# Two-step attention and a routed expert layer on one core: squared lengths off TensorE, PSUM banks given out singly, 1 MB stores and another order

## The chip, the core and the metric

The kernel runs on one core of a Trainium2 chip. The core has five engines that run side by side and each take their instructions in order: TensorE (PE; its weight loads are listed as PEld), VectorE (DVE), ScalarE (ACT), GpSimd (POOL) and SyncE (SP), which here only issues DMA transfers. ScalarE issues DMAs too. The working memory SBUF has 128 partitions; matmuls write to PSUM, eight banks of 512 float32 for each partition. The metric is the device time of one execution in microseconds (us).

## What is computed

```
h   = softmax(scale * I  @ x^T) @ x          # per batch b: 32 inducing rows over 11456 tokens
out = softmax(scale * x  @ h^T) @ h          # per token: over the 32 rows of h
xn  = out / (|out| + 1e-6);  en = emb / (|emb| + 1e-6)
logits = xn @ en^T / tau;    e = argmax(logits)      # 8 experts
gate   = softmax(logits)[e]
result = gate * (relu(out @ w1[e]) @ w2[e])
```

There are 4 batches of 11456 tokens with 128 channels, and 8 experts with a hidden width of 1024. Everything is float32.

## The kernel before

**What it works on.** A batch is cut into six pieces k of 2048 tokens (the last one of 1280). `xT` holds a piece with the channels on the partitions (1 MB), `x` holds it with the tokens on the partitions (two halves of 512 KB). For three pieces of batch 0 (`OWN`, `own`, line 345) x is not loaded but made on the chip from xT by transposes.

**Stage 1** (`stage1`, line 365) is the first softmax. For one or two pieces: scores by TensorE (`scores1`), a running maximum on VectorE (`mk`, `nb`), exponentials on ScalarE, transposes on TensorE, a copy on ScalarE, and the matmuls with x (line 448), added up in `hj`. `finish` (line 463) combines the four row groups into h transposed (`hT`, lines 514 to 520), finds the likeliest expert from the sum of the rows of h, has its weights w1 and w2 loaded by SyncE (`load`, line 543), and calls `tables`, which makes `HB` (the products of the rows of h with each other) and `gbd` (the products of the rows of h with the normalised expert vectors, in columns of a weight matrix, beside a column of ones).

**Stage 2** (`stage2`, line 587) is done for each piece k, 16 tiles of 128 tokens: scores (line 604), the maximum over 32 rows and its spreading by two transposing instructions (`mx`, `mxb`, lines 611 and 614), the difference (line 619), the exponential e (line 622). The length of an output token needs the sum over rows of e times (HB e). So TensorE computes HB e (line 623), VectorE multiplies it with e into `q` (line 625), and TensorE adds q up with the weights `nnb` into the same bank in which it adds e up with the weights `gbd` (function `half`, lines 630 and 631; two matmuls each). One transposing copy `gat` (line 643) brings the sums back with the tokens on the partitions, in `gts`.

**The gate** (`gate`, line 648) follows after three, two or one pieces (`GATES`): inverse square root by logarithm and exponential with one Newton step on GpSimd, logits, softmax, argmax. It is a chain of some fifteen small operations that goes to and fro between VectorE, ScalarE and GpSimd, and it ends in `f`, the factor of each token. If every hidden unit keeps its sign over all tokens, w1 and w2 fold into one matrix `L` for each batch (`fold`, line 748); `check` (line 815) tests whether that holds, and collects what has to be done again.

**Stage 3** (`stage3`, line 890): f is spread (line 873, VectorE), multiplied with e (line 875, GpSimd: `pf`), multiplied with L (line 901, TensorE, four matmuls into two PSUM tiles `pc` of two banks), copied out in halves (line 914, ScalarE) and stored in halves of 512 KB (`put`, line 884, issued by ScalarE).

**Order.** The whole program is a straight list of instructions whose order a planner sets while the program is built (`Plan`, line 77). Every step is added with an engine, an assumed duration, its dependences, the buffers it takes and frees, and a priority: the slot's time plus a constant of the stage (`PA`, `PT`, `PX`, `PC`, `PF`, `PD`). `run` picks, again and again, the step that can begin first; on one engine those that can begin within 0.2 us of each other go by priority. Buffers are rings (`BUFS`): the next user of a ring gets the oldest buffer. PSUM is two such rings, `pb` (four single banks) and `pc` (two pairs). Where TensorE would wait over 0.6 us for work that has a buffer already, matmuls on zeros are put in (`fill`, line 977).

**Behind the plan**, `worklist` (line 938) makes the list of what has to be done again, its count is read into registers on every engine (line 1055), and a loop over the list follows (line 1059). For the inputs here the list is empty, and the loop's body isn't run.

## Time and profile before

| | |
|---|---|
| median of three runs | 270.82 us (269.31 to 272.33) |
| the profiled execution | 271.37 us, of which its span 269.7 us |
| TensorE in the chain that ended last | 45% of the span |
| transfers in that chain | 22% |
| VectorE in that chain | 20% |
| moved by DMA | 72.29 MB, 268 GB/s on average |
| read from HBM, written | 48.13 MB, 23.72 MB |

The profile's first part gives each engine's busy time, share and number of instructions. The slices divide the span into 40 equal parts; a digit is tenths, and PEclk is the clock granted to TensorE. A row of stretches gives, for each piece of time, its length, the busy time of each engine with the number of instructions, the granted clock (1.00 is full speed), the share of the DMA engines and the GB/s that they moved. A row of instruction groups reads: line, engine, operation, what is written from what with its shape, the count, then busy us and mean ns, then the engine's idle time before these instructions and what ended it. A timeline row gives start, length, engine, line, and in brackets the idle time before it. A float32 matmul leaves two records, so "x8" stands for four matmuls.

### The profile page before, as it was taken

What the parts mean: (1) busy time and instruction counts of PE and PEld (TensorE: products, weight loads), DVE (VectorE), ACT (ScalarE), POOL (GpSimd) and SP (SyncE); (2) the same over time, 40 slices, a digit from 0 to 9 for tenths busy, and PEclk for the clock granted to TensorE, in tenths of its full rate; (3) what the DMA queues carried; (4) which work ended last, traced back from release to release, by engine and by line L of the source; (5) the groups of instructions that cost most, each with busy time, mean ns of one, the idle gap of its engine ahead of it and who ended that gap; (6) DMA issues with size and microseconds to landing.
All of it is one profiled execution on the core that took longest, in us unless ns stands there. A gap on an engine that the chain in (4) does not pass through costs nothing.

```text
span 269.7 us, 5435 instructions
## 1 busy us (share of the span) xinstructions
PE 225.8 (84%) x1993; PEld 122.0 (45%) x1993; DVE 179.1 (66%) x524; ACT 105.5 (39%) x227; POOL 68.9 (26%) x128
## 2 busy tenths in 40 slices
PE   8989899589968999999499998977996899786540
PEld 2557454246535256654273645633631564342220
DVE  5545247943897667979369869589589637958520
ACT  2355330131411472263016542666465720155430
POOL 2000000000440114641001353623257204263700
PEclk9999999979996699999959999999999799999755
DMA  6999998994781999859919998274579640037460
GB/s 187 397 419 384 399 377 317 402 395 159 260 304 36 314 382 418 364 203 368 419 53 277 385 417 359 85 293 172 214 231 417 255 173 0 0 156 289 173 252 17
DMA packets 18690, 72.29 MB, mean 268 GB/s; under 512 B 2456, under 2 KB 2976, under 8 KB 16224
## 3 DMA queue, kind: packets, MB, share of 16 engines
q1 hardware_dynamic: 11392, 48.37, 48.1%
q10 hardware_dynamic: 7264, 23.49, 21.8%
q8 instruction: 18, 0.29, 0.4%
q14 instruction: 16, 0.13, 0.2%
HBM read 48.13 MB, written 23.72 MB: 266 GB/s over the span
## 4 chain that ended last, share of the span: by engine, by line
PE 45%; DMA 22%; DVE 20%; ACT 4%; issue 3%; POOL 2%; ACTq 1%; DVEq 0%; POOLq 0%
DMA xT<-in_xT 18%; PE pc L901 9%; PE pb L630 6%; PE pb L631 5%; PE pb L604 5%; PE pb L623 5%; PE pb L448 4%; PE pc L331 3%; ACT o L914 3%; DMA out<-o 3%; PE pc L426 2%; DVE fb L873 2%; DMA itau<-in_tau 2%; DVE mk L388 2%; DVE gm L479 1%
## 5 line engine op out<-in xcount | busy, mean ns | idle before, releaser
L914 ACT COPY o<-pc 128x512 f32<-128x512 f32 (+1 forms) x94 | 48.3, 564 | 37.5 <-PE pc L901 26.8
L875 POOL TENSOR_TENSOR pf<-e,fb 128x512 f32<-128x512 f32 (+1 forms) x24 | 29.0, 1214 | 36.6 <-PE pc L901 14.8
L901 PE MATMUL pc<-pf,L 32*128 32x512 f32 (+1 forms) x192 | 32.7, 669 | 6.7 <-ACT o L914 3.9
L623 PE MATMUL pb<-e,HB 128*128 128x512 f32 (+1 forms) x48 | 25.0, 603 | 3.7 <-ACT o L914 2.2
L622 ACT ACTIVATE e<-d 128x512 f32<-128x512 f32 (+1 forms) x24 | 14.5, 603 | 23.1 <-DVE R L619 16.6
L331 PE MATMUL pc<-xT,indT_sb 128*32 128x512 f32 x120 | 16.6, 639 | 8.0 <-DMA xT<-in_xT 7.9
L604 PE MATMUL pb<-xT,hT 128*32 128x512 f32 x160 | 21.6, 640 | 0.0
L403 ACT ACTIVATE s<-pc,nb 128x1024 f32<-128x1024 f32 (+1 forms) x9 | 9.5, 1058 | 29.2 <-DVE nb L395 19.2
L643 DVE STREAM_TRANSPOSE gts<-pb 128x256 f32<-128x256 f32 (+1 forms) x24 | 10.3, 428 | 15.1 <-PE pb L631 14.9
L611 DVE TRANSPOSE_TENSOR_REDUCE mx<-pb 128x16 f32<-128x512 f32 (+1 forms) x24 | 16.1, 671 | 5.7 <-PE pb L604 5.7
L448 PE MATMUL pb<-x,pt 128*32 128x128 f32 x608 | 19.6, 274 | 0.1
L448 PEld LDWEIGHTS pb<-x,pt 128*32 128x32 f32 x608 | 16.0, 110 | 7.9 <-issue 3.2
L901 PEld LDWEIGHTS pc<-pf,L 32*128 32x128 f32 x192 | 10.7, 198 | 18.8 <-issue 10.2
L625 DVE TENSOR_TENSOR q<-pb,e 128x512 f32<-128x512 f32 (+1 forms) x24 | 15.4, 644 | 4.5 <-PE pb L623 4.3
L630 PE MATMUL pb<-q,nnb 128*128 128x256 f32 (+1 forms) x48 | 15.7, 410 | 1.8 <-DVE q L625 1.4
L614 DVE STREAM_TRANSPOSE mxb<-mx 128x512 f32<-128x512 f32 (+1 forms) x24 | 16.1, 670 | 0.4
L619 DVE CUSTOM_DVE_ANT_0 d<-mxb,pb 128x512 f32<-128x512 f32 (+1 forms) x24 | 15.5, 646 | 1.2
L388 DVE TENSOR_REDUCE mk<-pc 128x1 f32<-128x1024 f32 (+1 forms) x9 | 10.2, 1139 | 8.9 <-PE pc L331 8.0
L630 PE MATMUL pb<-e,gbd 128*128 128x256 f32 (+1 forms) x48 | 15.5, 407 | 0.4 <-DVE R L619 0.4
L873 DVE STREAM_TRANSPOSE fb<-f 128x512 f32<-128x512 f32 (+1 forms) x24 | 15.4, 658 | 0.3
L631 PE MATMUL pb<-e,gbd 128*128 128x256 f32 (+1 forms) x48 | 14.6, 387 | 0.0
L631 PE MATMUL pb<-q,nnb 128*128 128x256 f32 (+1 forms) x48 | 14.4, 384 | 0.0
(202 smaller groups left out, 359.7 us busy)
## 6 DMA issues: line engine op xcount, KB each, us to landing
out<-o ACTq DMA_DIRECT2D x40, 512.0 KB, 3.0
xT<-in_xT SPq DMA_DIRECT2D x19, 1024.0 KB, 12.4
x<-in_xP SPq DMA_DIRECT2D x38, 512.0 KB, 10.4
xL<-in_xT SPq DMA_DIRECT2D x4, 640.0 KB, 12.9
w1t<-in_w SPq DMA_DIRECT2D x4, 512.0 KB, 4.6
w2t<-in_w SPq DMA_DIRECT2D x4, 512.0 KB, 5.8
out<-o ACTq DMA_DIRECT2D x4, 320.0 KB, 2.5
out<-o ACTq DMA_DIRECT2D x4, 288.0 KB, 2.5
```

Source lines behind the costliest of these rows:

```text
L331: nc.tensor.matmul(ps[32 * j:32 * j + 32, :].rearrange("p (g i) -> p g i", i=128), lhsT=indT_sb, rhs=v[:, j], start=True, stop=True)
L448: nc.tensor.matmul(ph.t[32 * j:32 * j + 32, 0:C], lhsT=pt.t[:tw, tat[k] + g, 32 * j:32 * j + 32], rhs=x, start=k == ks[0] and g == 0, stop ...
L604: nc.tensor.matmul(ps[32 * j:32 * j + 32, :W].rearrange("p (t i) -> p t i", i=32), lhsT=st.hT[:, 0:M], rhs=v[:, j], start=True, stop=True)
L611: nc.vector.tensor_reduce(t["mx"][:, :T], b1.t[:, :W].rearrange("p (t i) -> p t i", i=32), AX.X, ALU.max, apply_transpose=True)
L614: c(DVE, t_dve(W), lambda: nc.vector.transpose(new(mxb)[:, :W], t["mx"][:, :T].unsqueeze(2).broadcast_to([P, T, 32])), take=[mxb])
L623: o = c(PE, t_pe(W), lambda: nc.tensor.matmul(new(b2)[:, :W], lhsT=st.HB, rhs=e.t[:, :W], start=True, stop=True), take=[b2], deps=[st.do.g ...
L630: nc.tensor.matmul(b3.t[:, :H], lhsT=w[:, 16:], rhs=src.t[:, :H], start=kw["start"], stop=False)
L631: nc.tensor.matmul(b3.t[:, :H], lhsT=w[:, :P], rhs=src.t[:, H:W], start=False, stop=kw["stop"])
L873: c(DVE, t_dve(W), lambda: nc.vector.transpose(new(fb)[:, :W], st.f[k].unsqueeze(3).broadcast_to([P, 2, T // 2, 32])), take=[fb], deps=[st ...
L875: c(POOL, t_pool(W), lambda: nc.gpsimd.tensor_tensor(new(pf)[:, :W], st.e[k].t[:, :W], fb.t[:, :W], ALU.mult), take=[pf], free=[fb, st.e[k]])
L901: nc.tensor.matmul(pcs[j // 2].t[:, 512 * (j % 2):512 * (j % 2) + W], lhsT=st.L[32 * j:32 * j + 32, :], rhs=pf.t[32 * j:32 * j + 32, :W], ...
L914: (nc.vector.tensor_copy if dve else nc.scalar.copy)(v[:, 2 * i:2 * i + 2], src)
```

## The change

1. **Squared lengths.** q and its two matmuls with `nnb` are gone. ScalarE copies HB e from PSUM to SBUF (`keep_hq`), GpSimd multiplies it with e (`times`), and VectorE adds it up over 32 rows with a transposing sum (`squared`) straight into a buffer `nn`. The sums with `gbd` and `gat` stay, and no longer wait for q.
2. **The gate.** Its steps get their own dependences instead of one chain, and each waits in the plan for the same step of the gate before. nn's lower bound goes from VectorE to ScalarE (a Relu and a bias `tiny`), the sum `se` goes from one VectorE reduction to three additions on GpSimd (but for the last gate).
3. **The fold.** `Gm` is made on GpSimd (`chosen`), the sides' small sums `pa`, `na` on VectorE; they were the other way round.
4. **PSUM.** One tile of eight banks; the planner gives out single banks, or two neighbouring ones, to each user (`banks_for`). Stage 3 takes four single banks, and each copy frees one.
5. **Stores** of a whole piece (1 MB, 24 in all) from two buffers of 1 MB. The store of hT goes from SyncE's queue to ScalarE's.
6. **Order.** Every step has a name; its priority is the slot's time plus a number for that name from a table (`FIRST`), and from the last batch on a second one (`LATE`). The 0.2 us of choice becomes a number for each engine (`NEAR`). Steps of batch 0's first stage and its finish get priorities far below all others. Assumed durations are changed slightly. Waits for buffers that the plan hadn't known are added as dependences: `get_w` waits for the fold before, `seen` for the last check, `fix` for hj three steps before.
7. **The end.** The work list becomes steps of the plan. The loop stands in the else branch of a test for an empty list, with a branch hint.

The diff's core:

```diff
-BUFS = dict(xT=7, xL=2, x=6, xR=1, s1=2, pt=1, mxb=2, d=2, e=7, q=2, gts=2, lg=2, ex=1, fb=2, pf=2, o=4, pb=4, pc=2)
+BUFS = dict(xT=7, xL=2, x=6, xR=1, s1=2, pt=1, mxb=2, d=2, e=7, hq=2, gts=2, lg=2, ex=1, fb=2, pf=2, o=2, mx=2, nn=2, f=3)
+BANKS = 8
...
+NEAR = dict(PE=0.1, Activation=0.5, DVE=0.1, SP=1.5, Pool=0.7)
...
+        o.prio = when + FIRST.get(o.name, 0.0) + (LATE.get(o.name, 0.0) if when >= T0 + (NB - 1) * NSB * SLOT else 0.0)
...
+    def banks_for(self, o, t):
+        free = {i: at for i in range(BANKS) for at in [self.bank_at(i)] if at is not None}
+        out = []
+        for b in o.take:
...
+            for i in range(BANKS - b.n + 1):
+                if not all(i + j in free for j in range(b.n)):
+                    continue
+                at = max(free[i + j] for j in range(b.n))
+                near = sum(1 for j in (i - 1, i + b.n) if j in free and free[j] <= max(t, at))
+                key = (max(t, at), near, -at, i)
+                if best is None or key < best[0]:
+                    best = (key, i, at)
...
-        c(DVE, t_dve(W), lambda: nc.vector.tensor_tensor(new(q)[:, :W], b2.t[:, :W], e.t[:, :W], ALU.mult), take=[q], free=[b2])
...
-        c(PE, t_pe(W) + 0.1, lambda: half(nnb, q, start=False, stop=True), deps=[o], free=[q])
...
+        def keep_hq():
+            nc.scalar.copy(paired(new(hq)[:, :W]), halved(b2.t[:, :W]))
+        c(ACT, t_act(W), keep_hq, take=[hq], free=[b2])
+        def times():
+            nc.gpsimd.tensor_tensor(paired(hq.t[:, :W]), paired(hq.t[:, :W]), halved(e.t[:, :W]), ALU.mult)
+        c(POOL, t_pool(W), times)
+        def squared():
+            nc.vector.tensor_reduce(new(nn)[:, t0:t0 + T], hq.t[:, :W].rearrange("p (t i) -> p t i", i=32), AX.X, ALU.add,
+                                    apply_transpose=True)
+        o_nn = c(DVE, t_dve(W), squared, take=[nn] if t0 == 0 else [], free=[hq])
...
-            nc.vector.tensor_scalar(t["nn"], col(NC, 1)[:, :, 0], 1e-30, None, ALU.max)
...
+            nc.scalar.activation(t["nn"], nn.t[:, :T], AF.Relu)
+            nc.scalar.activation(t["r"], t["nn"], AF.Ln, bias=tiny)
...
-            nc.vector.tensor_reduce(se, t["ex"], AX.X, ALU.add)
...
+            nc.gpsimd.tensor_tensor(x[:, :, 0:4], x[:, :, 0:4], x[:, :, 4:8], ALU.add)
+            nc.gpsimd.tensor_tensor(x[:, :, 0:2], x[:, :, 0:2], x[:, :, 2:4], ALU.add)
+            nc.gpsimd.tensor_tensor(t["se"], x[:, :, 0], x[:, :, 1], ALU.add)
...
-            nc.vector.tensor_tensor(st.Gm, st.G, pos.unsqueeze(2).broadcast_to([P, NCH, M]), ALU.mult)
...
-            nc.gpsimd.tensor_tensor(pa, sa, ss, ALU.add)
-            nc.gpsimd.tensor_tensor(na, sa, ss, ALU.subtract)
...
+            nc.gpsimd.tensor_tensor(st.Gm, st.G, t["pos"].unsqueeze(2).broadcast_to([P, NCH, M]), ALU.mult)
...
+            nc.vector.tensor_tensor(pa, sa, t["ss"], ALU.add)
+            nc.vector.tensor_tensor(na, sa, t["ss"], ALU.subtract)
...
-        pcs = [plan.buf("pc") for _ in range(2)]
+        pcs = [plan.buf("ps") for _ in range(4)]
...
+        o = plan.buf("o")
+        for j in range(4):
+            def evict(j=j, dve=split and j % 2 == 1):
+                v = new(o)[:, :P * T].rearrange("c (t j i) -> c j t i", j=4, i=32)
+                (nc.vector.tensor_copy if dve else nc.scalar.copy)(v[:, j], pcs[j].t[:, :W].rearrange("c (t i) -> c t i", i=32))
...
+        st.do["out", k] = plan.add(ACT, 0.34, put_o, deps=ops, free=[o], when=when, size=P * P * T * 4)
...
-    ni = worklist()
-    n_items = nc.values_load(ni, min_val=0, max_val=NB * E)
+    n_items = nc.values_load(left["ni"], min_val=0, max_val=NB * E)
...
-    with tc.For_i(0, n_items, 1) as i:
+    tc.mark_branch_hint_location("none", "LikelyTaken", engines=ENGINES)
+    with tc.If(n_items == 0, preferred_fallthrough_block=False, label="none") as none:
+        pass
+    with none.Else():
+        with tc.For_i(0, n_items, 1) as i:
```

More of the change, by code (lines that the diff above doesn't have):

```diff
@@ L114, in ready_at @@
                 return None
-            t = max(t, d.end + (0.0 if d.eng == o.eng and not d.size else self.HOP))
+            t = max(t, d.end + (0.0 if d.eng == o.eng and not d.size else self.HOP + d.lag))
+        o.room = 0.0
         want = {}
-        o.room = 0.0
         for b in o.take:
+            if b.ring == "ps":
+                continue
             live = self.rings.setdefault(b.ring, [])
@@ L152, in run @@
             for b in o.take:
-                self.rings[b.ring].append(b)
+                if b.ring != "ps":
+                    self.rings[b.ring].append(b)
+            for b, i, _ in o.got if o.take and o.take[0].ring == "ps" else ():
+                b.at = i
+                for j in range(b.n):
+                    self.banks[i + j] = b
             for b in o.free:
@@ L498, in finish, with fin @@
         c(DVE, 0.2, zf)
[L499 removed]
+        def fin():
+            nc.tensor.matmul(new(b3)[:, 0:1], lhsT=flat(sel4), rhs=t["z"], start=True, stop=True)
+        c(PE, 0.3, fin, take=[b3])
         def selr():
@@ new lines, in expB, with hb @@
+        def expB():
+            nc.scalar.activation(new(e)[:, :W], d.t[:, :W], AF.Exp, scale=-SCALE)
+        o_e = c(ACT, t_act(W), expB, take=[e], free=[d])
+        def hb():
+            nc.tensor.matmul(new(b2)[:, :W], lhsT=st.HB, rhs=e.t[:, :W], start=True, stop=True)
+        c(PE, t_pe(W), hb, take=[b2], deps=[st.do.get("tab")])
+        halved = lambda v: v.rearrange("p (u t i) -> p t u i", u=2, i=32)
+        paired = lambda v: v.rearrange("p (t u i) -> p t u i", u=2, i=32)
+        def keep_hq():
+            nc.scalar.copy(paired(new(hq)[:, :W]), halved(b2.t[:, :W]))
@@ L640, in gat @@
+            nc.tensor.matmul(b3.t[:, :H], lhsT=st.gbd[:, :P], rhs=e.t[:, H:W], start=False, stop=True)
+        o = plan.add(PE, t_pe(W), sums, deps=[o_e, st.do.get("tab")], take=[b3], when=when)
         def gat():
@@ L690, in newton @@
                 nc.gpsimd.tensor_tensor(t["n"], t["n"], t["p"], ALU.mult)
-        c(*((DVE, 3 * dv()) if last else (POOL, 4 * po)), newton)
+        o_n = add(*((DVE, 3 * dv()) if last else (POOL, 4 * po)), newton, deps=[o_r])
         def den():
@@ L697, in den @@
             nc.vector.reciprocal(t["den"], t["den"])
-        c(DVE, dv() + 0.43, den)
+        o_d = add(DVE, dv() + 0.5, den, deps=[o_z, o_n])
         def lg():
@@ L702, in lg @@
             nc.gpsimd.tensor_tensor(t["lg"], col(0, E), b8(t["den"]), ALU.mult)
-        c(POOL, t_pool(E * T), lg, take=[lgb], free=[gts])
+        o_l = add(POOL, 0.12 + 0.00172 * E * T, lg, deps=[o_d], take=[lgb], free=[gts])
         def lm():
@@ L825, in check, with chk @@
         c(DVE, 0.2, rm, deps=[st.do["R", k] for k in range(NSB)])
-        c(PE, 0.3, lambda: nc.tensor.transpose(new(b1)[0:1, 0:P], t["rm"], ident), take=[b1])
+        def chk():
+            nc.tensor.transpose(new(b1)[0:1, 0:P], t["rm"], ident)
+        c(PE, 0.2, chk, take=[b1])
         def r1():
@@ L872, in weighted @@
         fb, pf = plan.buf("fb"), plan.buf("pf")
-        c(DVE, t_dve(W), lambda: nc.vector.transpose(new(fb)[:, :W], st.f[k].unsqueeze(3).broadcast_to([P, 2, T // 2, 32])), take=[fb],
-          deps=[st.do.get(("f", k))])
-        c(POOL, t_pool(W), lambda: nc.gpsimd.tensor_tensor(new(pf)[:, :W], st.e[k].t[:, :W], fb.t[:, :W], ALU.mult), take=[pf],
-          free=[fb, st.e[k]])
-        return pf
-    def halves(k):
-        h = n_tiles(k) // 2
-        return [(0, h), (h, h)]
-    def put(st, k, o, a, h):
-        lap = LAP if k == NSB - 1 and a == 0 else 0
-        t0 = FULL * k if k < NSB - 1 else NTOK - LAST
-        st.put(t0 + P * a + lap, P * h - lap, o[:, lap:P * h])
@@ L890, in stage3, with spread_f, weigh, put @@
-    def stage3(plan, st, k, prio, split=False):
+        def spread_f():
+            nc.vector.transpose(new(fb)[:, :W], st.f[k].unsqueeze(3).broadcast_to([P, 2, T // 2, 32]))
+        c(DVE, t_dve(W), spread_f, take=[fb], free=[st.fv[k]], deps=[st.do.get(("f", k))])
+        def weigh():
+            nc.gpsimd.tensor_tensor(new(pf)[:, :W], st.e[k].t[:, :W], fb.t[:, :W], ALU.mult)
+        c(POOL, t_pool(W), weigh, take=[pf], free=[fb, st.e[k]])
+        return pf
+    def put(plan, st, k, o):
+        lap = LAP if k == NSB - 1 else 0
+        t0, n = (FULL * k, FULL) if k < NSB - 1 else (NTOK - LAST, LAST)
+        st.put(t0 + lap, n - lap, o[:, lap:n])
@@ L903, in stage3 @@
[L903 to L918 removed]
+                nc.tensor.matmul(new(pcs[j])[:, :W], lhsT=st.L[32 * j:32 * j + 32, :], rhs=pf.t[32 * j:32 * j + 32, :W], start=True, stop=True)
```

658 lines of the change are left out of this document (369 added, 289 removed).

## The prediction

> **What bounds the kernel now.** I read the page's busy times and slices first, then the busy times of five stretches that I cut by what the work is, then the waits and the timeline where a stretch shows a hole.
>
> ```profile
> span 269.7 us, 5435 instructions
> ...
> PE 225.8 (84%) x1993; PEld 122.0 (45%) x1993; DVE 179.1 (66%) x524; ACT 105.5 (39%) x227; POOL 68.9 (26%) x128
> ...
> PEclk9999999979996699999959999999999799999755
> ```
>
> TensorE is busy for 84% of the span. The share alone doesn't say where it is the limit, because part of it is filler (line 977: matmuls on zeros that keep the clock up). The stretches do:
>
> ```profile
> core 0: us, PE busy (x) PEld busy (x) DVE busy (x) ACT busy (x) POOL busy (x), PEclk, DMA share, GB/s
> ...
> 39.80:84.50 44.70, 37.68 (x388) 21.25 (x388) 32.28 (x79) 9.88 (x21) 6.78 (x12) 0.94 0.75 280
> 84.50:195.00 110.50, 101.27 (x945) 55.95 (x949) 83.23 (x226) 49.55 (x106) 33.51 (x57) 0.93 0.76 289
> 195.00:226.00 31.00, 26.61 (x160) 13.50 (x163) 20.80 (x55) 16.21 (x36) 11.53 (x22) 0.94 0.63 237
> 226.00:262.40 36.40, 24.22 (x129) 11.35 (x121) 24.44 (x80) 14.33 (x32) 15.15 (x25) 0.87 0.39 155
> 262.40:269.70 7.30, 0.00 (x0) 0.00 (x0) 0.00 (x0) 0.00 (x0) 0.00 (x0) 0.50 0.16 47
> ```
>
> Up to 39.8 us batch 0 is loaded and its first attention step ends. From 39.8 to 226 ("the middle", 186.2 us) stage 2 and 3 of one batch run beside stage 1 of the next. There TensorE is busy for 165.6 us. Only 0.8 us of it is filler:
>
> ```profile
> 84.50:195.00 110.50, 0.81 (x3) 0.29 (x3) 0.93 0.76 289
> ```
>
> So real TensorE work fills 164.8 / 186.2 = 88.5% of the middle. VectorE follows with 136.3 us (73%), then the transfers: shares 0.75, 0.76 and 0.63 make 137 us (74%). From 226 us on no engine is full, and the gate's steps and the last outputs wait for each other. The last 7.3 us hold no compute instruction at all. The executed run took 271.4 us, 1.7 around its span; the median of the runs, 270.8, is 0.2% less, so I sum against 271.4.
>
> **The change part by part.**
>
> *The squared lengths leave TensorE.* The two matmul pairs on q with the weights nnb (lines 630 and 631) go. In the middle they hold, by stretch:
>
> ```profile
> 39.80:84.50 44.70, 5.55 (x20) 3.56 (x20) 0.00 (x0) 0.00 (x0) 0.94 0.75 280
> 84.50:195.00 110.50, 13.98 (x52) 9.41 (x52) 0.00 (x0) 0.00 (x0) 0.93 0.76 289
> 195.00:226.00 31.00, 4.63 (x16) 3.28 (x16) 0.00 (x0) 0.00 (x0) 0.94 0.63 237
> ```
>
> That is 24.2 us, and leaves TensorE 140.6 us of work in the middle. If TensorE stayed the limit at 88.5%, the middle would take 158.9 us: 27.3 us less. That is the far end of the gain, because other engines get the work:
>
> ```profile
> L914 ACT COPY o<-pc 128x512 f32<-128x512 f32 (+1 forms) x94 | 48.3, 564 | 37.5 <-PE pc L901 26.8 <-ACT o L914 7.8 <-DMA out<-o 2.8
> ...
> L875 POOL TENSOR_TENSOR pf<-e,fb 128x512 f32<-128x512 f32 (+1 forms) x24 | 29.0, 1214 | 36.6 <-PE pc L901 14.8 <-DVE q L625 7.6 <-PE pb L554 5.8
> ...
> L611 DVE TRANSPOSE_TENSOR_REDUCE mx<-pb 128x16 f32<-128x512 f32 (+1 forms) x24 | 16.1, 671 | 5.7 <-PE pb L604 5.7
> ...
> L625 DVE TENSOR_TENSOR q<-pb,e 128x512 f32<-128x512 f32 (+1 forms) x24 | 15.4, 644 | 4.5 <-PE pb L623 4.3
> ...
> L864 POOL TENSOR_TENSOR seen<-seen 128x192 f32<-128x192 f32 (+3 forms) x16 | 6.2, 387 | 1.3
> ...
> L735 DVE TENSOR_REDUCE se<-ex 128x48 f32<-128x384 f32 (+3 forms) x9 | 4.3, 476 | 0.0
> ...
> L665 DVE TENSOR_SCALAR nn<-gts 128x48 f32<-128x48 f32 (+3 forms) x9 | 2.0, 221 | 0.3
> ...
> L779 DVE TENSOR_TENSOR Gm<-G,pos 128x256 f32<-128x256 f32 x4 | 1.8, 454 | 0.1
> ```
>
> ScalarE copies the product out of PSUM 24 times; by the eviction's 564 ns that is 13.5 us. GpSimd multiplies it with e 24 times, by the 1214 ns of its other multiplication of that size 29.1 us. VectorE drops q (644 ns) and takes the transposed sum "squared" (by mx, 671 ns): 24 x 27 ns = +0.6. It also drops nn (2.0) and the sum se, except the last one (about 4.1); six of nine gates lie in the middle, so 6/9 x 6.1 = -4.1. Gm goes to GpSimd: -1.8. The sums of se become three GpSimd additions, by line 864's mean 3 x 0.39 = 1.2 us for each of eight gates. pa and na come from GpSimd to VectorE, eight small operations of about 0.16 (the row of line 858 below): +1.3. GpSimd ends near 69 + 29 + 9 = 107 us and ScalarE near 119: half of a shorter span, so neither is the limit by its sum.
>
> *GpSimd's operations hold up VectorE's.* This is in the trace already:
>
> ```profile
> 77.79 1.27 POOL L875 TENSOR_TENSOR pf<-e,fb 128x512 f32<-128x512 f32 x1 [2.48 <-DVE fb L873]
> ...
> 77.90 1.24 DVE L479 COPY gm<-gm 1x128 f32<-1x128 f32 x1
> ...
> 118.48 0.88 POOL L875 TENSOR_TENSOR pf<-e,fb 128x320 f32<-128x320 f32 x1
> ...
> 118.58 0.84 DVE L696 SCALAR_TENSOR_TENSOR den<-zz,n 128x48 f32<-128x48 f32 x1
> ```
>
> A copy of one row takes 1.24 us and ends with the multiplication on GpSimd beside it; so does the short den. Two such pairs cost VectorE about 1.6 us over what an instruction this small needs (the 0.16 of line 858). With 38 us more on GpSimd I add 3 us to VectorE in the middle, and between nothing and 10 for the range: nothing if the new multiplications meet only PSUM readers, 10 if one in three of some 32 new GpSimd pieces holds one small operation up for its whole 1 us. [...]
>
> So VectorE's work in the middle becomes 136.3 + 0.6 - 4.1 - 1.8 + 1.3 + 3 = 135.3 us, close to TensorE's 140.6, with the transfers at 137 unchanged. Three equal loads don't reach TensorE's 88.5%. VectorE's best long stretch is
>
> ```profile
> 140.00:195.00 55.00, 49.79 (x493) 27.55 (x489) 43.42 (x119) 29.15 (x62) 19.59 (x31) 1.00 0.71 269
> ```
>
> 79% over 55 us, with TensorE full beside it. I take 80%, since TensorE now leaves room: 135.3 / 0.80 = 169 us, **17 us less**. The ends are 27 (TensorE's share kept) and 1 (VectorE keeps the 73% of the whole middle: 135.3 / 0.732 = 185).
>
> *Banks given out one by one, and the new order.* In the start, batch 0's last steps were interleaved with batch 1's:
>
> ```profile
> 32.20 0.35 DVE L459 SCALAR_TENSOR_TENSOR hj<-hj,fix,pb 128x128 f32<-128x128 f32 x1 [2.07 <-PE pb L448]
> ...
> 33.78 0.08 PEld L470 LDWEIGHTS pb<-ident,nb 128*1 128x1 f32 x1 [0.84 <-issue]
> ...
> 33.92 1.22 DVE L388 TENSOR_REDUCE mk<-pc 128x1 f32<-128x1024 f32 x1 [1.37 <-PE pc L331]
> ...
> 35.06 0.27 DVE L474 TENSOR_REDUCE gm<-pb 1x32 f32<-1x128 f32 x1
> ```
>
> The transpose of line 470 could have run at 32.55 and came at 33.78; its minimum was ready at 34.05 and waited behind mk until 35.06. The new priorities put all of batch 0 first: **2.2 us less** (0 to 4: its loads stay the limit before). The same kind of hole, a load at the head of TensorE's queue, is in the middle:
>
> ```profile
> 133.10 1.45 PE L331 MATMUL pc<-xT,indT_sb 128*32 128x512 f32 x8 [3.63 <-DMA xT<-in_xT]
> ```
>
> I count its 3.6 us in the 80%, not again. The end:
>
> ```profile
> 251.59 1.07 ACT L914 COPY o<-pc 128x512 f32<-128x512 f32 x2 [0.64 <-PE pc L901]
> ...
> 255.08 0.16 DVE L858 TENSOR_TENSOR present<-present,wipe 128x1 f32<-128x1 f32 x1
> ...
> 255.87 1.07 ACT L914 COPY o<-pc 128x512 f32<-128x512 f32 x2 [1.72 <-PE pc L901]
> ...
> 259.51 0.75 ACT L914 COPY o<-pc 128x320 f32<-128x320 f32 x2 [1.08 <-PE pc L901]
> ...
> 260.01 0.89 DVE L914 COPY o<-pc 128x320 f32<-128x320 f32 x2 [4.77 <-ACT o L914]
> ...
> 262.36 0.35 SPq L966 DMA_DIRECT2D items<-li  x1
> ```
>
> One output's evictions begin 4.28 and 3.64 us after the other's, because the next matmuls need the four banks that are being emptied. With eight banks they run ahead, and four copies and an issue set the pace, 4 x 0.59 + 0.34 = 2.7: 2.5 us less. The work list, whose input is complete at 255.24, no longer follows the last output: the last instruction moves from 262.36 to the last eviction's end, 260.90: 1.4 less. Against it, the last gates' chain gets longer: copy, multiplication and sum take 0.56 + 1.21 + 0.67 = 2.4 us where q, the matmul pair and gts took about 2.2; se takes 0.8 more; and the multiplication can wait for one of line 875 before it, 0.6 on average, with 0.2 for the added Relu: about 1.8 in all.
>
> *Stores of 1 MB.* Half the issues on ScalarE's queue, the same bytes.
>
> ```profile
> out<-o ACTq DMA_DIRECT2D x40, 512.0 KB, 3.0
> ...
> out<-o ACTq DMA_DIRECT2D x4, 288.0 KB, 2.5
> ```
>
> A store now starts after all four copies instead of two, and two buffers of 1 MB stand where four halves stood. With outputs every 2.7 us, the third output of a group waits for the first store: it is issued at 3, lands 4 to 5 us later (3.0 for half the bytes), and the third's copies would begin at 5.4. That is about 1.6 us in the end; in the middle ScalarE's idle time hides it, and if that cover went it would cost 1.6 for each of six groups, 10 us. The end makes -2.5 - 1.4 + 1.8 + 1.6 = **0.5 us less** (5 less to 4 more).
>
> *The closing loop* gets a branch around it with a hint. Of the 7.3 us after the last instruction, at least the last store's landing stays (2.5): the gain lies between 4.8 and a loss of 1 for the added branch. I take **1 us less**, near the side on which nothing happens.
>
> Sum: 271.4 - 17 - 2.2 - 0.5 - 1 = 250.7, and 0.2% for the median: **250 us**.
>
> **The rivals.**
> 1. TensorE stays the limit and the order packs the rest around it: 271.4 - 27.3 - 3.7 = 240. For it speaks the 88.5% reached before; against it that VectorE would have to run at 135.3 / 158.9 = 85% throughout, above its 79%.
> 2. VectorE and the chain over four engines (copy, multiply, sum) take TensorE's place: the middle gains 1.4 and the total is 266. For it speak the blocked pairs above; against it the nearly full TensorE beside VectorE's 73%.
> 3. Slower: the lighter TensorE loses its clock. The slices show it at 0.5 to 0.6 after holes (the slices that begin at 80.9 and 134.8 us), and 0.87 from 226 on. The middle ran at a mean of 0.934. 140.6 us at 0.934 becomes 175 at 0.75, and at 88.5% the middle takes 198: 12 more, 279 in all. It decides below a mean of 0.78, where the middle takes 190. Against it speaks that the filler is still planned into holes over 0.6 us. [...]
> 4. The transfers hold the pace: the holes at loads (3.6 us at 133) grow by what TensorE saves, and the middle stays at 186. 269, within 1%. Against it speaks that transfers are at 74% there.
>
> **How the numbers follow.** My forecast (about 242 to 260) has 0.62, rival 1 0.15, rival 2 0.10, rival 3 0.07, rival 4 0.06. About 1% either way, 268 to 274, can't be told from no change: faster 0.86, same 0.07, slower 0.07. Leaving out what lies beyond rival 1 with its best end and beyond rival 2, the range is 236 to 266.
>
> **What would show it.** The nnb rows gone and TensorE's busy time lower by some 26 us. VectorE's share of the middle at 80% or more (forecast), 73% (rival 2), TensorE's at 88% (rival 1). A granted clock below 0.8 in the middle would show rival 3; load waits before line 331's matmuls longer than 8 us in sum, rival 4. [...] Batch 0's line of hT before 38 us, evictions 2.7 us apart in the end, and less than 7.3 us after the last instruction would show the small steps. I'm wrong if the order leaves holes that the 80% doesn't allow for, or fills those that I counted as unavoidable.

## The result, and the profile after

The changed kernel takes 237.81 us (median of four runs, 236.28 to 240.33), the kernel before on the same chip 270.06 (267.25 to 272.33). The ratio is 0.882, with a 95% interval from 0.868 to 0.895: 32 us less. Executions more than 1.5% above the fastest of their kernel are left out of the ratios, but not of the medians. The time lies within the range on record (236 to 266), but outside the forecast itself (242 to 260, a chance of 0.62): it is that of rival 1 (240), in which TensorE stays the limit and which had 0.15. The profiled execution took 236.28 us, the shortest of the four, and that of before 271.37: this pair is 35 us apart.

The head of the profile of the changed kernel answers to the one shown of before:

```profile
span 234.5 us, 5142 instructions
...
PE 198.0 (84%) x1861; PEld 102.7 (44%) x1861; DVE 179.4 (76%) x512; ACT 118.2 (50%) x260; POOL 108.0 (46%) x172
...
PEclk9999997999999979999996799999976999859555
```

TensorE lost 27.8 us of busy time (8.7 of it filler, which fell from 17.3 to 8.7 us, most of it in the start and the end), VectorE's stayed, ScalarE (118.2) and GpSimd (108.0) grew to what the prediction's sums gave (119 and 107). TensorE's share of the span is 84% as before: the span shrank with its work. Cut at about the same work as before (start, middle, end, tail), the stretches of the changed kernel read (length, busy time of each engine with the number of instructions, clock, DMA share, GB/s):

```profile
0.00:40.00 40.00, 33.36 (x368) 19.73 (x369) 18.27 (x87) 14.77 (x34) 1.94 (x12) 0.96 0.95 360
40.00:197.10 157.10, 146.31 (x1393) 74.81 (x1391) 137.72 (x357) 85.14 (x183) 86.17 (x127) 0.95 0.82 317
197.10:228.30 31.20, 18.29 (x102) 8.17 (x102) 23.37 (x69) 18.32 (x44) 19.89 (x34) 0.71 0.57 235
228.30:234.50 6.20, 0.00 (x0) 0.00 (x0) 0.00 (x0) 0.00 (x0) 0.00 (x0) 0.50 0.32 112
```

The middle went from 186.2 to 157.1 us (29.1 less), the end from 36.4 to 31.2, the tail from 7.3 to 6.2, and the start not at all. The cut between middle and end isn't quite at the same work: behind it the changed kernel still has one more piece of stage 3 and the last fold's matmuls (line 956), and has the last scores done. Cut at one instruction that both have, the copies of the first and the last hT (39.8 and 194.9 us before, 40.0 and 175.4 after), the stretch between them is 19.7 us shorter, and the rest up to the last instruction 14.6. Filler in the middle is small again, so TensorE's real work there is 146.3 - 1.4 = 144.9 us, or 92% of the stretch, and VectorE's 137.7 us is 88%:

```profile
40.00:197.10 157.10, 1.42 (x5) 0.29 (x3) 0.95 0.82 317
```

Why could VectorE rise from 73% to 88% with the same work? Its waits in the middle tell it (who waited for whom, us in total, times, the longest). First the kernel before, then the changed one:

```profile
DVE gts L643 <- PE pb L631: 14.5, 11, 2.9
DVE mk L388 <- PE pc L331: 6.7, 2, 4.4
DVE mx L611 <- PE pb L604: 5.7, 7, 2.4
DVE q L625 <- PE pb L623: 3.8, 8, 0.9
DVE den L696 <- POOL n L690: 3.7, 3, 2.2
```

```profile
DVE mk L485 <- PE ps L425: 2.5, 2, 1.8
DVE mx L722 <- PE ps L716: 2.0, 2, 1.7
DVE HB L692 <- PE ps L687: 1.9, 2, 1.3
DVE hT L626 <- PE ps L621: 1.8, 1, 1.8
DVE gts L774 <- PE ps L767: 1.7, 3, 0.9
```

Before, VectorE stood still because it waited for TensorE: 30.7 us in the first four rows, nearly half of it at line 631, the very matmuls that were removed. In the changed kernel all five rows together are 9.9 us.

### The profile page after: what moved, and what is told of

Read it like the earlier page. It is cut to its first block, busy times and chain, and to the rows that moved or that the text cites. A ratio compares the mean times of both kernels' runs of the same rounds, so it can differ in the third digit from the quotient of the medians.

```text
span 234.5 us, 5142 instructions
## 1 busy us (share of the span) xinstructions
PE 198.0 (84%) x1861; PEld 102.7 (44%) x1861; DVE 179.4 (76%) x512; ACT 118.2 (50%) x260; POOL 108.0 (46%) x172
## 4 chain that ended last, share of the span: by engine, by line
## 5 line engine op out<-in xcount | busy, mean ns | idle before, releaser
L754 POOL TENSOR_TENSOR hq<-hq,e 128x512 f32<-128x512 f32 (+1 forms) x24 | 29.0, 1211 | 69.0 <-ACT hq L750 69.0
L1072 ACT COPY o<-ps 128x512 f32<-128x512 f32 (+1 forms) x94 | 47.6, 569 | 20.4 <-PE ps L1065 14.0
L1065 PE MATMUL ps<-pf,L 32*128 32x512 f32 (+1 forms) x192 | 35.5, 736 | 6.6 <-POOL pf L1046 6.6
L425 PE MATMUL ps<-xT,indT_sb 128*32 128x512 f32 x160 | 21.2, 602 | 6.6 <-DMA xT<-in_xT 6.4
L744 PE MATMUL ps<-e,HB 128*128 128x512 f32 (+1 forms) x48 | 24.9, 609 | 0.3 <-DVE g L644 0.3
L738 ACT ACTIVATE e<-d 128x512 f32<-128x512 f32 (+1 forms) x24 | 14.5, 602 | 20.0 <-DVE R L733 18.8
L716 PE MATMUL ps<-xT,hT 128*32 128x512 f32 x160 | 23.1, 681 | 1.5 <-DVE hT L626 1.5
L750 ACT COPY hq<-ps 128x512 f32<-128x512 f32 (+1 forms) x24 | 13.4, 558 | 20.0 <-PE ps L744 14.6
L546 PE MATMUL ps<-x,pt 128*32 128x128 f32 x608 | 20.8, 287 | 0.2 <-ACT pt L530 0.2
L546 PEld LDWEIGHTS ps<-x,pt 128*32 128x32 f32 x608 | 17.2, 115 | 6.8 <-issue 2.7
L722 DVE TRANSPOSE_TENSOR_REDUCE mx<-ps 128x16 f32<-128x512 f32 (+1 forms) x24 | 16.0, 667 | 2.1 <-PE ps L716 2.0
L766 PE MATMUL ps<-e,gbd 128*128 128x256 f32 (+1 forms) x48 | 15.0, 395 | 0.7 <-DVE R L733 0.7
L767 PE MATMUL ps<-e,gbd 128*128 128x256 f32 (+1 forms) x48 | 13.9, 373 | 0.0
```

Of the source, the lines that this page charges most:

```text
L425: nc.tensor.matmul(ps[32 * j:32 * j + 32, :].rearrange("p (g i) -> p g i", i=128), lhsT=indT_sb, rhs=v[:, j], start=True, stop=True)
L546: nc.tensor.matmul(ph.t[32 * j:32 * j + 32, 0:C], lhsT=pt.t[:tw, tat[k] + g, 32 * j:32 * j + 32], rhs=x, start=k == ks[0] and g == 0, stop ...
L716: nc.tensor.matmul(ps[32 * j:32 * j + 32, :W].rearrange("p (t i) -> p t i", i=32), lhsT=st.hT[:, 0:M], rhs=v[:, j], start=True, stop=True)
L722: nc.vector.tensor_reduce(new(mx)[:, :T], b1.t[:, :W].rearrange("p (t i) -> p t i", i=32), AX.X, ALU.max, apply_transpose=True)
L744: nc.tensor.matmul(new(b2)[:, :W], lhsT=st.HB, rhs=e.t[:, :W], start=True, stop=True)
L754: nc.gpsimd.tensor_tensor(paired(hq.t[:, :W]), paired(hq.t[:, :W]), halved(e.t[:, :W]), ALU.mult)
```

## The experiments

Kernels that are planned anew get another order of instructions than the changed kernel's; this had to be priced by itself (third and fourth experiment below). Where "own order" is written, the list of instructions is the changed kernel's, and only the named ones differ. The kernel before was run beside each group of experiments, with medians of 269.3 to 270.1 us; the changed kernel has only the four runs above.

### Undoing the move of the squared lengths, and making it alone

*old lengths*: in the changed kernel, q and the matmuls with nnb are back, all else stays.

```diff
-        c(ACT, t_act(W), keep_hq, take=[hq], free=[b2])
...
-        c(POOL, t_pool(W), times)
...
-        o_nn = c(DVE, t_dve(W), squared, take=[nn] if t0 == 0 else [], free=[hq])
...
+        o_q = c(DVE, t_dve(W), times, take=[hq], free=[b2])
...
+        o = plan.add(PE, t_pe(W), squared, deps=[o, o_q], free=[hq], when=when)
```

> The changed kernel with the squared lengths as before: VectorE multiplies into q, TensorE adds q up with nnb; the order is planned anew with the new tables. Theory (TensorE was the limit and still is, and the 24 us taken from it are the gain): TensorE's middle gets its 24 us back, 24 / 0.92 = 26 us more, some 262 us. Rival (the new order and the banks make the gain): most of it stays, 245 us or less. A third, both: 250 to 256.

Measured: 268.19 us, ratio to the kernel before 0.997 (0.991 to 1.004). That is nearest to the theory, and 6 us beyond it. Planned like this, priorities, banks, stores and the gate's moves together are worth nothing that can be measured while TensorE has its old work (223.9 us busy).

*before, new lengths*: in the kernel before, the move alone.

```diff
-        c(DVE, t_dve(W), lambda: nc.vector.tensor_tensor(new(q)[:, :W], b2.t[:, :W], e.t[:, :W], ALU.mult), take=[q], free=[b2])
...
+        c(ACT, t_act(W), lambda: nc.scalar.copy(paired(new(q)[:, :W]), halved(b2.t[:, :W])), take=[q], free=[b2])
+        c(POOL, t_pool(W), lambda: nc.gpsimd.tensor_tensor(paired(q.t[:, :W]), paired(q.t[:, :W]), halved(e.t[:, :W]), ALU.mult))
...
-        c(PE, t_pe(W) + 0.1, lambda: half(nnb, q, start=False, stop=True), deps=[o], free=[q])
```

> The kernel before with nothing but the squared lengths' move (ScalarE copy, GpSimd multiplication, VectorE sum); rings, priorities, stores and gate as before. Theory: some 24 / 0.885 = 27 us less, about 245. Rival (without the new order the longer chain over four engines eats it): 258 to 272.

Measured: 287.10 us, ratio 1.066 (1.058 to 1.073): slower by 18, which is beyond both sides of the expectation. The longest of VectorE's waits in this kernel's middle, and then that stretch itself:

```profile
DVE nn L631 <- POOL q L628: 16.8, 10, 5.0
```

```profile
41.50:243.00 201.50, 163.65 (x1432) 84.27 (x1431) 138.36 (x364) 86.93 (x183) 78.19 (x113) 0.86 0.67 256
```

VectorE waits 16.8 us for GpSimd's product; in the changed kernel the same sum (line 758) has no idle time before it. TensorE is busy for 81% of the stretch, and at a clock of 0.86 (0.94 in the middle of before), so a part of the loss may be clock; how much isn't shown. This is what rival 2 describes, in the old order: the chain over four engines takes TensorE's place as the limit. Neither part alone makes the kernel faster, both together give 32 us. The move takes work from the limit and makes the chain longer; something in the rest of the change lets that chain run ahead.

### How much hangs on the exact order

*other order*: the changed kernel, planned anew with one assumed duration of the planner changed by 0.01 us.

```diff
-t_dve = lambda w: 0.13 + w / 960
+t_dve = lambda w: 0.14 + w / 960
```

> The changed kernel, planned with VectorE's assumed duration 0.01 us longer for each instruction; the instructions are the same, their order and the banks come out a little different. Theory (the tables are good for this instruction list in general, so what old_priorities and split_banks lost is the worth of the tables and of the free banks): 236 to 243. Rival (the recorded order is a lucky hit of the search, and any other plan loses): 246 or more, and then the 18 us of old_priorities and the 20 us of split_banks are no price of a part.

Measured: 248.13 us (247.72 to 249.16), ratio 0.926 (0.918 to 0.933): 10 us are lost with the same instructions (but for some filler), and the rival of the expectation came. (The tables of priorities are the result of a search, as the expectation says.) Its middle, cut at about the same work, and its end:

```profile
39.80:205.00 165.20, 154.18 (x1387) 78.13 (x1385) 133.97 (x351) 87.47 (x191) 85.36 (x125) 0.90 0.78 304
205.00:241.20 36.20, 23.82 (x132) 10.49 (x131) 24.51 (x74) 15.61 (x37) 20.68 (x36) 0.79 0.50 191
```

TensorE is busy for 93% of this middle as well. The middle is 8.1 us longer, and TensorE's busy time in it 7.9 us: nearly the same matmuls ran at a granted clock of 0.90 instead of 0.95. Length times clock is 149 in both (165.2 x 0.90, 157.1 x 0.95). By this cut, what the searched order saves in the middle is clock. By the other one, from the first to the last hT, 135.4 us at 0.95 stand against 145.3 at 0.91, which is 129 against 132: there clock makes some 6 of the 10 us, and the rest doesn't come from it. Behind the middle, the end is 5 us longer.

*before, other order*: the kernel before, nudged likewise.

```diff
-t_dve = lambda w: 0.15 + w / 960
+t_dve = lambda w: 0.17 + w / 960
```

> The kernel before with one number of its planner changed: VectorE's assumed duration is 0.17 us plus a part by width instead of 0.15. The steps, buffers and priorities are the same; only the order that the planner finds differs. For the changed kernel such a nudge cost 10 us. Theory that the kernel before was fitted to its order as closely: some 280 us, so that orders found without a search differ by 280 to 248, and the search's share is the same on both sides. Rival, that only the changed kernel's order is a hit: 266 to 274 us, and then 10 of the 32 us are owed to the search of the order alone.

Measured: 276.51 us, ratio 1.029 (1.019 to 1.040): 7 us are lost here too, between the two sides of that expectation: the kernel before hangs on its order as well, somewhat less than the theory had it. With nudged orders on both sides the change is worth 276.5 - 248.1 = 28 us, with found ones 32. One nudge on each side is a small sample; the sizes 7 and 10 are no more than that.

Read with the nudged orders as the base, since the undone parts were planned anew too: the base is 276.5, the move alone 287.1 (+10.6), the rest alone 268.2 (-8.3), both 248.1 (-28.4). Alone they would add up to +2.3; together they give some 31 us more than that.

### Two parts of the rest

*old priorities*: no table of names; the constants of the stages and the 0.2 us of choice as before. *split banks*: four banks for single users and four for pairs and stage 3, as the two rings had it.

```diff
-NEAR = dict(PE=0.1, Activation=0.5, DVE=0.1, SP=1.5, Pool=0.7)
+NEAR = dict(PE=0.2, Activation=0.2, DVE=0.2, SP=0.2, Pool=0.2)
...
-    stage1(plan, sts[0], n, EARLY * (ks[-1] - 10))
+    stage1(plan, sts[0], n, 3.0 * n)
```

```diff
-            for i in range(BANKS - b.n + 1):
+            for i in (range(4) if b.n == 1 and not b.wide else (4, 6) if b.n == 2 else range(4, 8)):
```

> The changed kernel with the stage constants of before as priorities (no tables for names, 0.2 us of choice on every engine); everything else as changed. Theory: within 3% of the changed kernel, 236 to 245. Rival (the order is what lets VectorE reach 88% of the middle): 252 or more, VectorE's share of the middle back near 79%.

> The changed kernel whose planner may give single-bank users only banks 0 to 3, and pairs and stage 3's outputs only banks 4 to 7, as the two rings of before did. Theory: the banks matter in the end alone, 238 to 243. Rival (free banks let TensorE run ahead everywhere): 247 or more.

Measured: 255.68 us (253.29 to 258.20; ratio 0.944, 0.937 to 0.951) and 257.55 us (253.99 to 259.04). Against the changed kernel that is 18 and 20 us, but a new order alone costs about 10 of them. Both are in the range of their expectation's rival. What is left, 7.5 and 9.4, is no larger than the nudge itself, so I can't say more than that each part helps by at most about that much. VectorE is busy for 78% of the time between the first and the last hT with the old priorities, and for 80% with the split banks (87% in the changed kernel, 82% in *other order*).

These two runs say something else besides. Both have the move of the squared lengths, and both are some 30 us faster than *before, new lengths* (287.10), though one has the old priorities and the other the old split of the banks; in neither does VectorE's wait for GpSimd's product stand among its first seven waits. So neither the table of priorities nor the single banks are needed, each by itself, for the chain to run ahead. Which of the parts that both keep does it (the gate's own dependences, the rings for `mx`, `nn` and `f`, the waits that the plan now knows), or whether either of the two tested is enough, wasn't tested.

With the split banks, GpSimd waits longer for stage 3's matmuls to free its buffer, as these two rows of the waits say, of *split banks* and of the changed kernel:

```profile
POOL pf L1047 <- PE ps L1068: 28.1, 12, 7.1
```

```profile
POOL pf L1046 <- PE ps L1065: 10.2, 3, 6.3
```

### Which engine is the limit now

*more tensor*, in the changed kernel's own order: each group of sums gets two more matmuls that nobody reads.

```diff
+            for w in (st.gbd[:, 16:], st.gbd[:, :P]):
+                nc.tensor.matmul(b3.t[:, 256:256 + H], lhsT=w, rhs=e.t[:, :H], start=True, stop=True)
```

> The changed kernel in its own order, with two more matmuls of 256 columns beside each sums (into the unused half of that bank, read by nobody), 24 times, as many as the change removed; the plan doesn't know of them. TensorE gets about 24 us more. Theory (TensorE, at 92% of the middle, is still the limit): 20 to 28 us more, some 260. Rival (VectorE, at 88%, or the chain is the limit): at most 12 more, 250 or less.

Measured: 254.31 us (251.65 to 256.69), ratio 0.945 (0.933 to 0.957).

```profile
PE 214.1 (85%) x1957; PEld 119.3 (47%) x1957; DVE 179.2 (71%) x512; ACT 118.6 (47%) x260; POOL 107.6 (43%) x172
```

TensorE is busy for 16.1 us more, and the time is 16.5 us longer: one for one. Neither side of the expectation has this time, because the 24 us it counted on were too many: the 48 further matmuls hold TensorE for 16.1. One thing speaks against taking this alone as proof that TensorE is the limit: the copy `gat` waits for the further matmuls too, so they lengthen the chain as well. VectorE's wait for them:

```profile
DVE gts L776 <- PE ps L769: 14.7, 15, 2.4
```

In the changed kernel the same copy (line 774) waits 3.0 us for TensorE. For TensorE as the limit speaks that its share from the first to the last hT is 92% here (138.4 of 150.2 us) as in the changed kernel (93%), while VectorE's falls from 87% to 78%.

*times on vector*, own order: VectorE makes the 24 products instead of GpSimd.

```diff
-            nc.gpsimd.tensor_tensor(paired(hq.t[:, :W]), paired(hq.t[:, :W]), halved(e.t[:, :W]), ALU.mult)
+            nc.vector.tensor_tensor(paired(hq.t[:, :W]), paired(hq.t[:, :W]), halved(e.t[:, :W]), ALU.mult)
```

> The changed kernel in its own order, with the multiplication of the copied product by e on VectorE instead of GpSimd (24 x about 0.64 us there, 29 us less on GpSimd). VectorE would need 152 us in a middle of 157. If VectorE limits beside TensorE: 12 to 18 us more, 250 to 256. If it has room because TensorE limits: within 5 us, up to 243. If GpSimd's holding up of VectorE is dear, the waits saved give some of it back.

*no times*, own order: the product is left out, and ScalarE writes the squares of HB e in its place, so that the lengths are others.

```diff
-            nc.scalar.copy(paired(new(hq)[:, :W]), halved(b2.t[:, :W]))
+            nc.scalar.activation(paired(new(hq)[:, :W]), halved(b2.t[:, :W]), AF.Square)
...
-            nc.gpsimd.tensor_tensor(paired(hq.t[:, :W]), paired(hq.t[:, :W]), halved(e.t[:, :W]), ALU.mult)
+            pass
```

> The changed kernel in its own order without GpSimd's multiplication: ScalarE squares the product as it copies it, so the lengths are not those of the reference and the gate's values differ; nothing else is left out. GpSimd has 29 us less, and the chain of each length one step less. [...]

Measured: 240.91 us (240.12 to 242.16; ratio 0.899, 0.891 to 0.907) and 235.93 us (232.47 to 237.59; ratio 0.871, 0.858 to 0.885). The busy times of the two:

```profile
PE 199.5 (84%) x1861; PEld 103.3 (43%) x1861; DVE 186.7 (78%) x536; ACT 118.7 (50%) x260; POOL 80.4 (34%) x148
```

```profile
PE 199.7 (85%) x1861; PEld 103.6 (44%) x1861; DVE 175.8 (75%) x512; ACT 118.2 (50%) x260; POOL 79.5 (34%) x148
```

The 24 products hold VectorE for 15.1 us, but its busy time rises by 7.3 only: without GpSimd's products beside it, its other work got 7.8 us shorter. Without any products (*no times*) VectorE is busy for 3.6 us less, near the 3 us that the prediction added for the middle, an estimate; why the two experiments differ isn't shown. With 7.3 us more on VectorE the time is 3.1 us longer, with 3.6 less it is 1.9 shorter, both near the spread of the changed kernel's own runs (4 us). The first time is where its expectation puts it if VectorE still has room (up to 243). It is not far behind, but TensorE is the limit.

### Small steps

*half stores*, own order: two stores of half a piece in place of each one. *old loop*, own order: no test for an empty list around the loop, and no hint.

```diff
-        st.put(t0 + lap, n - lap, o[:, lap:n])
+        h = n // 2
+        st.put(t0 + lap, h - lap, o[:, lap:h])
+        st.put(t0 + h, n - h, o[:, h:n])
```

```diff
-    tc.mark_branch_hint_location("none", "LikelyTaken", engines=ENGINES)
-    with tc.If(n_items == 0, preferred_fallthrough_block=False, label="none") as none:
-        pass
-    with none.Else():
-        with tc.For_i(0, n_items, 1) as i:
+    with tc.For_i(0, n_items, 1) as i:
```

> The changed kernel, its order and its buffers kept, with two stores of half a piece (512 KB) in place of each one of 1 MB; ScalarE issues twice as many, both after all four copies. Theory that the stores' size has no price or gain of its own (the transfers move the same bytes, and ScalarE is busy for half of the span): within 1 us of the changed kernel, 237 to 239 us; each of 24 further issues holds ScalarE for 0.34 us, 8 us in all, which its idle time hides except in the end, where four of them lie on the path: 1 us. Rival that large stores are a part of the gain: 242 us or more.

> The changed kernel, its order kept, with the closing loop as in the kernel before: no test for an empty list around it and no branch hint. Theory that the branch gives the little that the tail of the profile shows (6.2 us after the last compute instruction in place of 7.0): 0 to 1.5 us more than the changed kernel, 238 to 239.5 us, all of it behind the last compute instruction. Rival that the branch gives more than the profile's span shows (the rest around the span of 1.7 us too): 2 us or more. Rival that the test costs: below 237 us.

Measured: 238.74 us (231.99 to 244.88) with half stores: no difference that six runs can show. 240.87 us (239.74 to 243.04; ratio 0.899, 0.893 to 0.905) with the old loop. Its last store is issued at 230.94 us, and 7.0 us follow until the end of its span, where the changed kernel has 6.2; the time around the span is 1.8 us in both. So 0.8 us goes with the branch; the rest of its 3 us stands ahead of the last store, in a run whose TensorE was busy for 200.9 us with the same matmuls.

*moved steps*, own order but for the places of eight steps, meant to beat the changed kernel:

```diff
+    for steps, behind in (scores[1:2], fins[1]), (rest, hT), (ends, ops[[o.name for o in ops].index("vals")]):
...
+        for o in steps:
+            order.remove(o)
+        i = order.index(behind) + 1
+        order[i:i] = steps
```

> The changed kernel with its own order of instructions, in which eight steps are moved by hand and nothing is planned anew. In the start the second half of batch 1's first scores goes behind the matmul of gmb, the maximum mk and nb behind sel, and the transposes of line 523 behind the matmuls of hT; in the end VectorE's two copies of the last output go ahead of the work list's steps. Theory: in the start of the changed kernel these steps held up batch 0's chain by 1.65 us (score, 32.95 to 34.59), 0.9 us (mk) and 0.95 us (transposes), 3.5 us in all, so the copy of hT comes at 36.5 us instead of 40.0; TensorE is the limit from there on, so what the start gains comes through: 3 us. The last store is issued at 226.6 instead of 227.97 by the old clock: 1 us more. Together 233 to 235 us, 3 to 4 less than the changed kernel. Rival: the loads of batch 1 are late already, so that the start's gain turns into longer waits for xT in the middle, and the end waits for the work list's own transfer: hT comes early too, but the time is within 1 us of the changed kernel's.

Measured: 240.29 us (237.63 to 241.40), ratio 0.891 (0.885 to 0.897): nothing gained. The start's timeline of the changed kernel (start, length, engine, line, idle before), and then that of this one (its profiled execution took 241.40 us, the longest of the six):

```profile
33.59 1.07 PE L425 MATMUL ps<-xT,indT_sb 128*32 128x512 f32 x8 [1.25 <-DMA xT<-in_xT]
...
34.59 0.38 PE L584 MATMUL ps<-ones,gm 1*128 1x1 f32 x2
34.79 1.22 DVE L485 TENSOR_REDUCE mk<-ps 128x1 f32<-128x1024 f32 x1 [1.89 <-PE ps L425]
...
35.93 0.15 DVE L589 COPY gmb<-ps 128x1 f32<-128x1 f32 x1
...
36.13 0.94 PE L1157 MATMUL ps<-wz 128*128 128x512 f16 x2 [1.17 <-DVE gmb L589]
...
37.56 1.97 PE L523 MATMUL ps<-ident,s 128*128 128x128 f32 x8 [0.27 <-ACT s L500]
...
39.32 0.55 PE L620 MATMUL ps<-sel,hj 128*128 128x128 f32 x2
...
40.02 0.29 DVE L626 COPY hT<-ps 128x128 f32<-128x128 f32 x1 [1.82 <-PE ps L621]
```

```profile
35.76 0.49 PE L620 MATMUL ps<-sel,hj 128*128 128x128 f32 x2 [0.97 <-DVE sel L614]
36.09 0.28 PE L621 MATMUL ps<-selr,hj 128*128 128x1 f32 x2
38.38 1.97 PE L523 MATMUL ps<-ident,s 128*128 128x128 f32 x8 [2.01 <-ACT s L500]
40.14 1.06 PE L1157 MATMUL ps<-wz 128*128 128x512 f16 x2
41.00 0.63 PE L686 MATMUL ps<-hT 128*128 128x128 f32 x2
```

hT was copied at 36.9 instead of 40.0 us, as expected. But I had put batch 1's transposes (line 523) right behind hT's matmuls. Their input came 2.01 us later, and the tables (line 686), which need only hT, stood behind them: they ran at 41.00, where the changed kernel has 40.37. TensorE ran at half speed from 37.3 to 44.1 us. In the end the last store's issue moved ahead of the list's, so that the list's transfer is what the end waits for. The mechanism of neither side of the expectation was the one: the step was put in the wrong place. The transposes behind the first scores of stage 2 weren't tried.

## Why the prediction was right or wrong

| Term | predicted | measured |
|---|---|---|
| middle | -17 (ends -27 and -1) | -29.1 |
| start | -2.2 | +0.2 |
| end | -0.5 | -5.2 |
| behind the last instruction | -1 | -1.1 |

The measured terms are those of the profiled pair (35 us), and middle and end hang on the cut between them. The total is within the range because the range took in rival 1; the middle gained more than the far end given for it.

**The middle: TensorE stayed the limit, and neither the ceiling on VectorE nor the removed work was sized right.** VectorE's work came out as worked out: 137.7 us measured, 135.3 predicted. The step that failed is "VectorE's best long stretch is" 79%, "I take 80%". That stretch had TensorE full beside it, so its 79% was no ceiling of VectorE: it was TensorE's limit, seen in VectorE's idle time. The waits show it (14.5 us for line 631 alone). In the changed kernel VectorE's share is 88%, and TensorE's 92% beats even the 88.5% that rival 1 kept. The prediction held against rival 1 that VectorE would need 85%; it got more. *more tensor* and the two experiments on GpSimd's product fit TensorE as the limit, and that rival's time, 240, is the one that came.

But it came by two errors that cancel. The term "24.2 us" was too large: TensorE's real work in the middle fell from 164.8 to 144.9 us, by 19.9, not to 140.6. Rows of neighbouring matmuls overlap in the trace, so the time of one group isn't what goes with it:

```profile
222.06 0.59 PE L631 MATMUL pb<-q,nnb 128*128 128x256 f32 x2
222.49 1.02 PE L623 MATMUL pb<-e,HB 128*128 128x512 f32 x2
```

The first ends at 222.65, 0.16 us after the second has begun. At one such overlap for each of the 22 groups in the middle (88 records, four to a group) that is 3.5 of the missing 4.3 us (an estimate from these rows). More work than rival 1 counted, at a higher share than it counted (144.9 / 157.1 = 92%, not 140.6 / 158.9 = 88.5%), gave nearly its time. That TensorE lost "some 26 us" as foreseen is chance too: without filler it lost 19.2 (208.5 to 189.3).

**GpSimd holding up VectorE** was sized a little low: +3, an estimate, was predicted for the middle; in the whole kernel, without GpSimd's products VectorE's busy time is 3.6 us shorter in *no times*, and its other work 7.8 us shorter in *times on vector*. Single operations show how it comes about. The timeline of the changed kernel, and then that of *times on vector*, where the same operation has nothing beside it on GpSimd:

```profile
113.80 0.88 POOL L754 TENSOR_TENSOR hq<-hq,e 128x320 f32<-128x320 f32 x1
...
113.99 0.76 DVE L888 SCALAR_TENSOR_TENSOR f<-v,vp,se 128x48 f32<-128x48 f32 x1
```

```profile
116.45 0.27 DVE L888 SCALAR_TENSOR_TENSOR f<-v,vp,se 128x48 f32<-128x48 f32 x1
```

0.76 us instead of 0.27, and it ends within 0.1 us of GpSimd's product. Taken over all 24 products, 3.6 to 7.8 us are 0.15 to 0.33 us each. A long read of PSUM wasn't stretched: in the kernel before the maximum at 110.60 us (line 388, `mk` from `pc`, 128x1024) lay wholly beside two products on GpSimd (110.23 to 112.73) and took 1.19 us, where the six of its size take 1.21 on average. (A slip beside it: the two blocked pairs of the prediction cost 1.8 us over 0.16 each, not 1.6.)

**The start: wrong.** The step that failed is "The new priorities put all of batch 0 first". They don't reach far enough: the planner picks the step that can begin first, and batch 1's scores could. In the timeline above, the second half of the scores (line 425, waiting 1.25 us for its load) still stands ahead of line 584, mk ahead of gmb, and line 523 ahead of line 620. *moved steps* shows that those were what held hT back: 3.1 us.

**The end: right in part.** The evictions now begin 2.86 and 3.18 us apart, 2.7 was predicted:

```profile
219.62 2.05 ACT L1072 COPY o<-ps 128x512 f32<-128x512 f32 x4 [0.23 <-PE ps L1065]
...
222.48 2.05 ACT L1072 COPY o<-ps 128x512 f32<-128x512 f32 x4 [0.80 <-PE ps L1065]
...
225.66 0.76 ACT L1072 COPY o<-ps 128x320 f32<-128x320 f32 x2 [1.13 <-PE ps L1065]
...
227.00 0.89 DVE L1072 COPY o<-ps 128x320 f32<-128x320 f32 x2 [0.15 <-issue]
227.97 0.34 ACTq L373 DMA_DIRECT2D out<-o  x1
```

The output at 225.66 waits for its matmuls, not for a store: the 1.6 us predicted for that stayed away, since the outputs come a little further apart than assumed. (*half stores* has a wait of 1.07 us there.) The work list isn't last any more, as predicted, but its small steps run on VectorE ahead of the last copies (227.00). The evictions give 1.9 us (2.5 predicted), the work list at most 1.4, as predicted. For the remaining two us, and for what the longer chain of the gates cost (1.8 predicted), I have no row that stands alone, and some of it is the cut.

The end could be shorter still: its granted clock is 0.71, where before had 0.87. Where it was 0.50, the matmuls of an output took nearly twice as long as at 1.00 in the middle (first a row of the end, then one of the middle):

```profile
205.27 2.09 PE L1065 MATMUL ps<-pf,L 32*128 32x512 f32 x8 [1.25 <-POOL pf L1046]
```

```profile
146.23 1.14 PE L1065 MATMUL ps<-pf,L 32*128 32x512 f32 x8
```

**The loop and the stores**: 1.1 us less behind the last instruction, of which *old loop* gives the branch 0.8; the stores' size changes nothing that the six runs of *half stores* can show. A store of 1 MB landed 3.9 us after its issue (median of 20), where 4 to 5 was predicted.

**The rivals.** Rival 2 is real, but only where the rest of the change is missing (*before, new lengths*). Rival 3, a lost clock, is behind six to eight of the 10 us lost in *other order*, though it never decided the sign there: the mean in the middle was 0.95 in the changed kernel and 0.90 in *other order*, far over the 0.78 from which it would (0.86 in *before, new lengths*). Rival 4 fell: waits for loads of xT in the middle are 2.9 us in sum (7.2 before), while the transfers' share rose from 0.74 to 0.82. By the terms of the other rivals its time would have been 268, not 269.

**One thing missing**: the prediction added the parts up. They don't add: alone, the move of the squared lengths costs 18 us, and the rest gives nothing.

## What to carry to other kernels

A share of 79% on the second engine isn't its ceiling while the first engine is full (it was 88% after the change): look at what it waits for, and if that is the limiting engine, let the share rise with it. Taking work off the limit and giving it to a chain over other engines can pay only together with changes that let the chain run ahead (which of them did it here is open); tried alone, either half may look useless or harmful. Busy times of overlapping rows don't subtract (24.2 us by the rows, 19.9 by the stretches). And a plan found by search was worth 10 us (4%) over one neighbour here and 7 us (3%) in the kernel before, so compare a changed kernel with others that are planned anew, too, before a part's worth is read from undoing it.

## What the runs showed of the hardware

The granted clock decides more than was expected, and it was lost behind holes of two us and less. The start of *moved steps* and of the changed kernel show it; first these eight microseconds of the changed kernel, then of *moved steps* (the last columns are the clock, the DMA share and the GB/s):

```profile
36.00:44.00 8.00, 7.60 (x78) 5.19 (x81) 4.29 (x21) 2.40 (x4) 0.00 (x0) 0.79 0.67 257
```

```profile
36.00:44.00 8.00, 5.99 (x32) 3.83 (x35) 2.34 (x12) 2.22 (x3) 0.00 (x0) 0.58 0.63 243
```

Cut into half microseconds, the clock is 1.00 or 0.50 in both, except where it changes. So a mean of 0.79 over 8 us is 3.4 us at half speed, one of 0.58 is 6.7 us. Ahead of the first stand holes of 1.25 and 1.17 us on TensorE (the rows at 33.59 and 36.13 above). In *moved steps* a hole of 0.97 us ends at 35.76, and the clock fell 0.9 us into the next one, which lasts 2.01 us and ends at 38.38:

```profile
36.50:37.00 0.50, 0.00 (x0) 0.00 (x0) 0.47 (x3) 0.00 (x0) 0.00 (x0) 1.00 1.04 418
```

```profile
37.50:38.00 0.50, 0.00 (x0) 0.00 (x0) 0.00 (x0) 0.50 (x1) 0.00 (x0) 0.50 1.05 418
```

How much idle time it takes, and over how long, these two places don't show.

The filler's part: in the kernel before TensorE ran nothing but filler from 3.2 to 7.8 us, and the granted clock was 1.00 there. No kernel without filler was run, so what the filler saves isn't shown.

With the same matmuls in the same order, or nearly, TensorE's busy time then goes with the run's time: 198.0 and 236.3 us in the changed kernel's profiled execution, 200.0 and 238.5 with half stores, 200.9 and 240.1 with the old loop, 202.2 and 241.4 with the moved steps.
